# A convolution and an attention interleaved on one core: bound rows on the SyncE queue, a fourth convolution output tile, a new stored order

## Chip, cores and metric

The kernel runs on one core of one Trainium2 chip. The metric is the device time of one execution in microseconds; the kernel before takes 321.3 us (median of 3 runs, 320.46 to 322.23). The profile is one execution of the same kernel, with a span of 318.7 us.

## The reference

Two independent computations, whose outputs stand side by side in the last dimension (all inputs bf16, sequence S = 2048, width D = 640):

```python
def _A_ref(q, k, v, shift_k, ssm_k, ssm_D):          # H3 convolution
    k_shift = sum over t < 4 of k_pad[:, t:t+S] * shift_k[:, 3-t]
    kv = k_shift * v
    y = irfft(rfft(kv padded to 2S) * rfft(ssm_k padded to 2S))[:, :S]
    y = y.astype(bf16) + kv * ssm_D
    return q * y

def _B_ref(x, wq, wk, wv, wo, beta):                 # attention with memory
    # 32 heads of 20, N = 4 segments of L = 512 tokens
    for s in range(4):
        p = softmax(qs @ ks.T * scale + mask)
        a_dot = p @ vs
        a_mem = (phi(qs) @ M) / (phi(qs) @ z + 1e-6)
        outs[s] = g * a_mem + (1 - g) * a_dot        # g = sigmoid(beta)
        M, z = M + phi(ks).T @ vs, z + sum(phi(ks))
    return concat(outs) @ wo

return concatenate([a, b], axis=-1)
```

## The kernel before

**The convolution (A)** runs over five blocks dp of 128 channels. A Fourier transform is done as matmuls with constant tables (Wf forward, Wi inverse) and butterflies on VectorE. `load_sk` (388 to 396) brings the filter: GpSimd loads it into a buffer of the ring kT, VectorE copies it into a second order, and SyncE transposes that copy into another kT buffer; the ring has two buffers (n=2), so a copy has to wait until the last reader of the buffer two turns earlier is done. `load_kv` (398 to 407) brings v (tile vt, on GpSimd, on ScalarE for the first block) and the transposed k (tile kr, four transposes on SyncE). Then come `kshift` (diagonal matmuls, product with vt), the forward transforms "X" and "K" with butterflies `bfly`, `pointwise`, `ybfly`, and `inverse` (501 to 513): for each of four c it takes a tile from the ring outa, eight matmuls fill a PSUM bank, VectorE multiplies by q (tile qd, loaded by `load_q` on GpSimd) into outa, and GpSimd sends outa to HBM. Stage c of block dp is called A.dp.20 to A.dp.23 here.

**The attention (B)** runs over eight units u: segment s = u // 2 and half = u % 2 of the heads. A unit has a projecting part P.u and an attending part T.u. P loads xT once per segment (four transposes on SyncE; the first segment through TensorE), and projects K, Q and V in four token tiles of three blocks of five matmuls (128x320 each); ScalarE copies K and Q into the tile KQ, which SyncE transposes into KQT. `bound` (564 to 583) gets a bound of the softmax: a maximum over K (kam, VectorE), a matmul with the absolute values of Q (qabs), a copy by ScalarE into bT (16 x 512), and four transfers that put the rows of bT into row 20 of each head's 32 rows of KQT. So the matmul of Q and K subtracts the bound by itself. `mem` (585 on) updates the memory M. T has four groups g of four heads, `attn(g)`: matmuls into the single PSUM tile st (2048 wide), an exponential by ScalarE into ET, matmuls with V and the memory, a reciprocal rr and products on VectorE into o_s. For half 1 there follow `outt` (four transposes on SyncE, o_s to oT) and `outproj` (672 to 682), whose output GpSimd sends out.

**The order.** Nothing is issued while the functions run. The `Recorder` (100 to 273) keeps 1393 operations with their dependences; `emit` (197) then issues them in the order of the list ORDER (692, decoded in 756), a permutation of the 1393 indices packed as text. Each engine, and each engine's DMA queue, goes through its own instructions in that order, without overtaking; semaphores hold it where data is missing. Thus a DMA issued by SyncE waits in SyncE until its data is ready, and what stands behind it waits too. All instructions bear the line of `emit`, L216, in the profile, so groups are told apart by their tiles. `take` (225) gives the PSUM banks: one st tile and four banks w. `ring` (374) hands out the buffers in turn.

Of the kernel before, what the change touches and what calls it, by code (L numbers as in the profile page):

```python
# [21 lines left out]
S = 2048; D = 640; C = 512; P = 1024  # L22
H = 32; DH = 20; NS = 4; L = 512; NG = 8
# [252 lines left out]
class K3:  # L276
# [104 lines left out]
    def a_chunks(self, dp):  # L381
        nc = self.nc
        V = nc.vector
        dsl = slice(128 * dp, 128 * dp + 128)
        Wf, Wi, ident = self.Wf, self.Wi, self.ident
# [28 lines left out]
        def kshift(b):  # L414
            def f():
                kr, vt = st["kr"], st["vt"]
                ps = self.bank("w")
                for c in range(4):
                    for t in range(4):
                        cc = (c - t) % 4  # L420
                        p0 = KPAD + 128 * b + (c - t - cc) // 4
                        nc.tensor.matmul(ps[:, 128 * c:128 * c + 128], lhsT=kr[:, 0, cc, p0:p0 + 128], rhs=st["skd"][:, t, :], start=(t == 0), stop=(t == 3))
                V.tensor_tensor(out=vt[:, b, :, :], in0=ps.rearrange("p (c d) -> p c d", d=128), in1=vt[:, b, :, :], op=ALU.mult)
            return f
# [76 lines left out]
        def inverse(c):  # L501
            def f():
                U, qd = st["U"], st["qd"]
                outa = self.ring("outa", [128, 4, 128], n=3)
                py = self.bank("w")
                pyv = py.rearrange("p (a h d) -> p a h d", a=2, h=2)
                for h in range(2):
                    for k in range(4):
                        i, j = k // 2, k % 2
                        nc.tensor.matmul(pyv[:, :, h, :], lhsT=Wi[:, k, c, 128 * h:128 * h + 128], rhs=U[:, 4 * i + c, 256 * j:256 * j + 256], start=(k == 0), stop=(k == 3))  # L510
                V.tensor_tensor(out=outa[:], in0=py.rearrange("p (b d) -> p b d", d=128), in1=qd[:, :, c, :], op=ALU.mult)
                nc.gpsimd.dma_start(out=self.out[:, dsl].rearrange("(b p c) d -> p c b d", b=4, c=4)[:, c], in_=outa[:])
            return f

        X = [(load_kv, 0.1)] + [(kshift(a), 1.5) for a in range(4)] + [(fwd("X", c), 2.0) for c in range(4)] + [(bfly("X"), 7.0)]
# [4 lines left out]
    def b_proj_chunks(self, u):  # L520
        nc = self.nc
        V = nc.vector
        s, half = u // 2, u % 2
        KQT, PqT, Va = self.KQT[half], self.PqT[half], self.Va[half]
# [39 lines left out]
        def bound():  # L564
            kam = self.ring("kam", [128, 4], f32)
            V.tensor_reduce(out=kam[:], in_=KQT[:, 0:4, :], axis=AX.X, op=ALU.max, apply_absolute_value=True)
            A = self.ring("A", [128, 4, 16])
            V.tensor_tensor(out=A[:], in0=self.sel[:], in1=kam[:, :, None].to_broadcast([128, 4, 16]), op=ALU.mult)
            if s > 0:
                nc.scalar.activation(out=PqT[:], in_=QT, func=ACTF.Exp)  # L570
                tq = self.ring("tq", [128, 4, L])
                V.tensor_scalar(out=tq[:], in0=QT, scalar1=1.0, scalar2=1.0, op0=ALU.add, op1=ALU.max)
                V.tensor_tensor(out=PqT[:], in0=PqT[:], in1=tq[:], op=ALU.min)
            qabs = self.ring("tq", [128, 4, L])
            V.tensor_scalar(out=qabs[:].bitcast(i16), in0=QT.bitcast(i16), scalar1=0x7fff, scalar2=None, op0=ALU.bitwise_and)
            pb = self.bank("w")
            for g in range(4):
                nc.tensor.matmul(pb[0:16, :], lhsT=A[:, g, :], rhs=qabs[:, g, :], start=(g == 0), stop=(g == 3))
            bT = self.ring("bT", [16, L])
            nc.scalar.copy(out=bT[:], in_=pb[0:16, :])  # L580
            for hl in range(4):
                r = 32 * hl + DH
                nc.gpsimd.dma_start(out=KQT[r:r + 1, 4:8, :], in_=bT[4 * hl:4 * hl + 4, :])

        def mem():
            src, dst = self.Mbd[half][s % 2], self.Mbd[half][(s + 1) % 2]
# [10 lines left out]

        ch = [(load, 0.1)] if half == 0 else []
        ch += [(proj(t), 3.0) for t in range(4)] + [(bound, 4.0)]
        if s < NS - 1:  # L600
            ch.append((mem, 1.5))
# [88 lines left out]
BANKS = {"st": (1, 2048), "w": (4, 512)}  # L690
SUMMED = ("X",)
ORDER = (
    'c-jrs0|O9d8wJpNpXa{Wwr$(CZQJH*%WbuVp|;GSwrtzxmTg<#cmBkQWJDq)gd-YaArfLDB4Qvqq97_N0LX&KFa$(^5Zj_!WQ%F>5F3e625}J0Vp(*{geVrrVpvK`Zt*RZ#YGBBU~w&;'
    'Ww!j5(UMwbWU>O53P~)BB|u7~MO7rTbe7&yBZH;3+?LnUT4Kv%`7DQ}K?Y>CY?j8-Aw6<hE-Pe7FvJpCRun)HB(kE&hx{mnf+%R&Eh&<r5-Oq!Dx<I!v2s@4idr!%ZiP`6LoFAwAv<y-'
    '4{{(U$|Em&S#KL=eXOqyw-Q#;2H0pDZxyVf4YCO~#s*q36h}#vKxquNZ)~ddv&r^@^|xtO4qw|S`_4*Xij}d_R?5m+HGE}bZG?Sq<Lq0jfjU;#s-q?*Ssm0xE!0MQWW<m5ll^SB?XHcq'
    '={C{s*e&}3-(xZ+p^8<tR%nFQsAQF`4cekHTA&%KS#wmk8rB32tSK5=1JtyJXo(h94=t@eezBQ01+}cUb;Jw%VlS<p)wfS}&+Z$%3qIRCYmXV$4)bk+EwpFW0iDqa&8)foYQNbldtj}s'
    'k+rtQ_S7C)2kU5U>?gFfPWIZq#Xp#c@mPro=!)4k$G$^1%(A&Q6+Q6WR^Yw0vk%tZenu0UhL0A!sZB>je`1}ji~Rz5B>xc+ysO3V$R5RKAUWLMS#)28M@WIkc!H-`VoPlyW@0XW#Ud=S'
    'd01>qF&{Pkcl#X+@Q2m%KdrIPMmO7Fe_32_;&ag57UMT;v=z1lv(O8@(FZ*d+hckhkLU4ynI-V$))zgjr~QGy@F)7AKbB!2R$4-@?vHGXCGs~`!?)U7du&lXns2hzpeOYtp4gN5UEIS1'
    '+(&mjL@dVPM(o69TLbe=SY-`;o2|C3*lxQp0I__BJ;P4hhDM&&)A?F#$9inW25iCKwhlXx+@IquULu9Rz;2}UcX)+=Y>lP&*T~>&ZI``4Dqm+qP|x?EzBlmowio-*(g$NGcH2jQZT%DW'
    '82K69y|wSPy1vi8U<BIuerx9kEVUoB_TIurVi5kuAv<iX`~W)pejGy@@8KQ1r|0lqp3!r9SFi2eJd@Y)PTs{cdlrw)Y@XdCa2RT`I%~1Hcl0Bc%bWTsi^x8n+nafBKW%-zpAW}jKj260'  # L700
    'm>u*(UW3Q2s2B5re!@=L*WTa1@i8duk(kHx`XC?WgMEMx@qC`&zd{j@%raiqhx!pe=EMBB7xZs%9Lq5lqcFlp`f&fszeXXy;OG3JAN6ux+;4aZFYh<~yjSpRZmj6neY79N31sz>Udm76'
    'jGy+ie#IxabE04NtA5Jk@{U*XM_$<<`w#xW@A?#fkB9yN)BS}1>p%KbKk5JZG#77q;4{DERalLcSe1t`8b?r>hcONZF~)EESTEpJ{1ndMo}Wf(kHWKv%Bp_fYco1uc{INDYMxic^~6gk'
    'pPqVd<<U6*$s6!zAMbCx4ww2bKEvy>Az%ADfA8n;yBAd=7E@xTVG1txMy$uQOv&fI#6S2)f8mW;pD+C)&f@}RdOXJGxBiDGV{%g8xydC>^2z?E|K-2>GXD>SR9MUXZ@+{D{LK^clS5~$'
    '7r*#tpXI5Tnn{?HSM9uAvg<b6=lJ)YjztuM8JV6LSXS5UvR$wnHrLNu6VCIdJZEtfSM$9Yn=`-4C^J{^Uo7yLT<DAZA1|j&EU2IYilBBZuZoJSN{XTiYR{Ugt%$0lT8gCW=)jJwrrylO'
    '8_3B{?962>t<}E5tE#@1v$FoR|17GiD3)R?n(C^at{}OZs-*tbDqrb;bGer3AO54hjIJ1JtgC3lR&2o(x?+8J(JmvNO6e9_Grrb%TP9UAHCIfvP!ruobtO<sCR0l#)LL()l-leoluBDX'
    'gL1Hj5-G7(Dx+5EFaF7_T*_?B&TD9`cKU-it*zQ93vc3guGdCo(rRteI%QUBrO{e$P;Ta719f8(b!S(0VOpirI_70V<zo-#XF(QV7Hw5l_2VE8W`FKgS9Q}i?a+R0*8%O*PIcE|4dDQ0'
    'Qx6U0Kz3Fa?NN5E(N|on0UE)9I;NE@${Z@hoJy~rT*aPR&Es0bUh1trI-y+Zr(xXa-*7$qY6Fj`kxr_=Hu)$H(nt=`V13OI8qSd#s)!+kNa1Tm2;V417^WgTs^J>VaU9FS9K%yOt<Bn^'
    'Q97tG8m&W`sF>kfMGIpUJ(T2lj?;L3rSm$Y<2<W#D#Z!>f#0bZcWIqZ(q!%AZmsw4^@ED@1n-~(H~21I&=g%%c}~?d{j2{JH^dJKLK(&jmy|3d36~WoL=DNq_dLbK;ii&?TS^rwa5ATG'
    'f~Ko1r*ay1bDQtsW^UnaUC|xw<vwort9qfA+Uxr~ZJ5q$`jOX_I;0CfGkwSq(u5!NleY7THgZ3A`!CwTr`qG2cvo9_U-xu?+xSe+^*}p(r)LbA!e>q5w=B(x{EjDCjun|TWC@u=w(vzi'
    '>mU#Fp&sc7f8sB^%4@vL|9FY-)n32xJU{58uJ8~$=!RzUu{vr7XYrL@>y6&(0x$A9Kj~j)4>y=2Ae<$`X%-9TSUjBJR-esXevC)?EB~KvQ0SyZT+EyySD4Q^%pFpMJfToX848D+yu~}b'  # L710
    '&AVK{dwjyDoXf|I6%vNXAyJ4OqJ$zLZ^##lhVr3AC>ctH{GoJs#&;?Zp7RA?vP>u#Ua>-`5o(4RDjR01T$robsu(JVIjR)qX{l<3+M!DLRljKo_xmHx<3rBZeLmnUEo7ZgH&hMP!fRF!'
    'Z@579LjAB%4MM}vC@j(+TCCsor{3{B-_q;@8;2(0Bfqd|aQj5q68)vmY#Ew|U@bzc&@8kG5v*-!7up9It#ycK9YW{OF?0)^LYL4ZbPrua&(JIU57-o<i~'
)


# [73 lines left out]
```

The softmax here doesn't subtract the row's maximum and nothing guards it: scores larger than these inputs give would overflow.

## Time and profile before

| Engine | busy, us | share | instructions |
|---|---|---|---|
| TensorE matmul (PE) | 285.8 | 90% | 5182 |
| TensorE weight load (PEld) | 208.1 | 65% | 5182 |
| VectorE (DVE) | 249.0 | 78% | 382 |
| ScalarE (ACT) | 259.1 | 81% | 347 |
| GpSimd (POOL) | 79.8 | 25% | 138 |

The largest groups by tile, with the mean of one:

| Group | count | busy, us | mean, ns |
|---|---|---|---|
| ACT exponential, ET from st | 96 | 154.3 | 1608 |
| PE projection, w from wqkv and xT | 480 | 76.6 | 306 |
| ACT copy, F from w | 80 | 45.0 | 608 |
| DVE butterflies, S from S | 40 | 37.1 | 945 |
| GpSimd issue of the rows, KQT from bT | 32 | 16.3 | 515 |
| GpSimd issue of outputs, out from outa | 20 | 15.9 | 794 |

SyncE's instructions are only DMA issues and are listed as SPq. The DMA queue of SyncE moves 21.85 MB in 76,800 packets and takes 43.5% of the 16 DMA engines' span, that of GpSimd 12.42 MB and 15.6%. A share of busy time is a mean over the whole span. Three views go further: the waits (how long an engine stood and what came last), the chain (which work ended last, followed back), and windows (busy time of every engine within a stretch). "PEclk" is the clock that TensorE was granted, 1.00 being full speed.

### The profile page before, as it was taken

What the parts mean: (1) busy time and instruction counts of PE and PEld (TensorE: products, weight loads), DVE (VectorE), ACT (ScalarE), POOL (GpSimd) and SP (SyncE); (2) the same over time, 40 slices, a digit from 0 to 9 for tenths busy, and PEclk for the clock granted to TensorE, in tenths of its full rate; (3) what the DMA queues carried; (4) which work ended last, traced back from release to release, by engine and by line L of the source; (5) the groups of instructions that cost most, each with busy time, mean ns of one, the idle gap of its engine ahead of it and who ended that gap; (6) DMA issues with size and microseconds to landing.
All of it is one profiled execution on the core that took longest, in us unless ns stands there. A gap on an engine that the chain in (4) does not pass through costs nothing.

```text
span 318.7 us, 11778 instructions
## 1 busy us (share of the span) xinstructions
PE 285.8 (90%) x5182; PEld 208.1 (65%) x5182; DVE 249.0 (78%) x382; ACT 259.1 (81%) x347; POOL 79.8 (25%) x138
## 2 busy tenths in 40 slices
PE   0789999999999999989999999199999989997984
PEld 0456777787578776757777766147767766764662
DVE  0264847899948899999989599295998999999970
ACT  0466689999997999999889999349988999987722
POOL 8000302700350011217300228200042243112443
PEclk9999999999999999999999999769999999997999
DMA  8899497699851877856091799935029681111264
GB/s 256 226 197 216 109 154 100 166 241 150 120 151 33 105 113 132 132 98 167 23 152 23 116 169 136 127 97 70 2 86 147 124 149 45 40 40 51 78 149 140
DMA packets 88115, 38.51 MB, mean 121 GB/s; under 512 B 78768, under 2 KB 84960, under 8 KB 87936
## 3 DMA queue, kind: packets, MB, share of 16 engines
q1 hardware_dynamic: 76800, 21.85, 43.5%
q0 software_dynamic: 5424, 12.42, 15.6%
q10 hardware_dynamic: 5840, 3.49, 3.7%
q8 instruction: 40, 0.66, 0.9%
q14 instruction: 11, 0.09, 0.1%
HBM read 14.15 MB, written 5.24 MB: 61 GB/s over the span
## 4 chain that ended last, share of the span: by engine, by line
PE 55%; DVE 20%; DMA 10%; ACT 8%; issue 4%; ACTq 1%; POOL 0%; SPq 0%; POOLq 0%; DVEq 0%
PE w L216 47%; PE st L216 8%; DVE S L216 7%; ACT ET L216 5%; DMA kT<-kT 5%; DVE o L216 2%; DMA o_s<-in_B_x_dram 2%; DMA oT<-o_s 2%; DMA KQT<-KQ 2%; DVE kam L216 2%; DVE pr L216 1%; DVE outa L216 1%; DVE tq L216 1%; DVE Kh L216 1%; DVE rr L216 1%
## 5 line engine op out<-in xcount | busy, mean ns | idle before, releaser
L216 ACT ACTIVATE ET<-st 128x2048 bf16<-128x2048 f32 (+1 forms) x96 | 154.3, 1608 | 10.8 <-PE st L216 9.5
L216 PE MATMUL w<-wqkv,xT 128*128 128x320 bf16 x480 | 76.6, 306 | 2.2 <-DVE xT L216 0.9
L216 PEld LDWEIGHTS <-xT 128*128 128x128 bf16 x480 | 45.1, 100 | 25.0 <-issue 6.7
L216 ACT CAST F<-w 128x512 bf16<-128x512 f32 x80 | 45.0, 608 | 12.0 <-PE w L216 11.6
L216 PEld LDWEIGHTS <-Wf 128*128 128x128 bf16 x400 | 36.1, 98 | 19.2 <-DMA out_dram<-outb 7.6
L216 PEld LDWEIGHTS <-ET 128*128 128x128 bf16 x1280 | 40.1, 96 | 7.3 <-issue 5.6
L216 PE MATMUL w<-Va,ET 128*128 128x21 bf16 x1280 | 43.0, 173 | 0.7 <-DVE outa L216 0.5
L216 POOL DMA_DIRECT2D KQT<-bT x32 | 16.3, 515 | 99.5 <-ACT bT L216 50.9
L216 DVE TENSOR_TENSOR S<-S 128x2048 bf16<-128x2048 bf16 (+1 forms) x40 | 37.1, 945 | 0.2
L216 PE MATMUL w<-vt,Wf 128*128 128x256 bf16 x240 | 35.5, 273 | 0.1
L216 PE MATMUL st<-KQT 21*128 21x512 bf16 (+3 forms) x512 | 34.4, 297 | 0.0
L216 PEld LDWEIGHTS <-later 32*128 32x128 bf16 x1536 | 18.8, 92 | 23.5 <-issue 21.1
L216 ACT CAST KQ<-w 128x320 bf16<-128x320 f32 x64 | 26.2, 435 | 8.3 <-PE w L216 6.8
L216 PE MATMUL st<-later 32*128 32x32 bf16 (+1 forms) x1536 | 27.0, 180 | 6.1 <-ACT ET L216 5.5
L216 PE MATMUL w<-kT,Wf 128*128 128x256 bf16 x160 | 23.5, 280 | 8.3 <-DMA kT<-kT 7.4
L216 PE MATMUL w<-wo,oT 128*128 128x320 bf16 x160 | 26.6, 309 | 2.0 <-DVE o L216 1.9
L216 POOL DMA_DIRECT2D out_dram<-outa x20 | 15.9, 794 | 44.4 <-DMA xT<-in_B_x_dram 26.5
L216 DVE TENSOR_TENSOR S<-Xh,Kh 128x4096 bf16<-128x4096 bf16 x10 | 22.9, 2286 | 0.1
L216 DVE TENSOR_REDUCE kam<-KQT 128x4 f32<-128x2048 bf16 x8 | 18.2, 2278 | 5.8 <-DMA KQT<-KQ 5.8
L216 ACT CAST outb<-w 128x320 bf16<-128x320 f32 x32 | 13.3, 443 | 10.0 <-PE w L216 7.8
L216 PEld LDWEIGHTS <-oT 128*128 128x128 bf16 x160 | 15.3, 100 | 8.9 <-issue 2.7
L216 POOL DMA_DIRECT2D qd<-in_A_q_dram x20 | 15.1, 757 | 23.6 <-DVE outa L216 17.5
(74 smaller groups left out, 432.6 us busy)
## 6 DMA issues: line engine op xcount, KB each, us to landing
qd<-in_A_q_dram POOLq DMA_DIRECT2D x20, 128.0 KB, 3.9
out_dram<-outa POOLq DMA_DIRECT2D x20, 128.0 KB, 3.1
out_dram<-outb POOLq DMA_DIRECT2D x16, 160.0 KB, 2.4
vt<-in_A_v_dram POOLq DMA_DIRECT2D x16, 128.0 KB, 3.6
kT<-in_A_ssm_k_dram POOLq DMA_DIRECT2D x4, 512.0 KB, 4.2
Wf<-c_wf ACTq DMA_DIRECT2D x4, 256.0 KB, 6.6
Wi<-c_wi SPq DMA_DIRECT2D x1, 1024.0 KB, 6.5
wo<-in_B_wo_dram SPq DMA_DIRECT2D x1, 800.0 KB, 6.9
```

The lines of the kernel that those rows point to most:

```text
L216: f(*fargs, **fkw)
```

## The change

Three edits. The four row transfers at the end of `bound` are issued by SyncE instead of GpSimd, 32 of 4 KB in all; their work and data stay the same. The ring outa gets a fourth buffer, so that a product of `inverse` waits for the output transfer four turns earlier instead of three. And the stored order is another one. It contains the same 1393 operations, so that every engine but SyncE and GpSimd issues exactly as many instructions as before, at other places; among the differences are the place of the filter transposes kT in SyncE's queue, the first loads of ScalarE, and the interleaving of A and B towards the end.

```diff
@@ inverse(c) @@
-                outa = self.ring("outa", [128, 4, 128], n=3)
+                outa = self.ring("outa", [128, 4, 128], n=4)
@@ bound() @@
             for hl in range(4):
                 r = 32 * hl + DH
-                nc.gpsimd.dma_start(out=KQT[r:r + 1, 4:8, :], in_=bT[4 * hl:4 * hl + 4, :])
+                nc.sync.dma_start(out=KQT[r:r + 1, 4:8, :], in_=bT[4 * hl:4 * hl + 4, :])
@@ ORDER @@
-    'c-jrs0|O9d8wJpNpXa{Wwr$(CZQJH*%WbuVp|;GSwrtzxmTg<#cmBkQWJDq)gd-YaArfLDB4Qvqq97_N0LX&KFa$(^5Zj_!WQ%F>5F3e625}J0Vp(*{geVrrVpvK`Zt*RZ#YGBBU~w&;'
...
+    'c-jTQ0{|FQ6a~<G-@AXdZQHhO+qT)v8f&)g)lgdvHP*b^YPP+aJ13G6iI5Ok5DAW0h=C}GhNy@DASNOrpaKlh5g9^Ei)xWAw#7zV#6dKRZkdo7Q7n$duvnHDDJ_*Hw-grNQXw7^SX_%|'
...
```

More of the change, by code (lines that the diff above doesn't have):

```diff
@@ L692 @@
 ORDER = (
-    'c-jrs0|O9d8wJpNpXa{Wwr$(CZQJH*%WbuVp|;GSwrtzxmTg<#cmBkQWJDq)gd-YaArfLDB4Qvqq97_N0LX&KFa$(^5Zj_!WQ%F>5F3e625}J0Vp(*{geVrrVpvK`Zt*RZ#YGBBU~w&;'
-    'Ww!j5(UMwbWU>O53P~)BB|u7~MO7rTbe7&yBZH;3+?LnUT4Kv%`7DQ}K?Y>CY?j8-Aw6<hE-Pe7FvJpCRun)HB(kE&hx{mnf+%R&Eh&<r5-Oq!Dx<I!v2s@4idr!%ZiP`6LoFAwAv<y-'
-    '4{{(U$|Em&S#KL=eXOqyw-Q#;2H0pDZxyVf4YCO~#s*q36h}#vKxquNZ)~ddv&r^@^|xtO4qw|S`_4*Xij}d_R?5m+HGE}bZG?Sq<Lq0jfjU;#s-q?*Ssm0xE!0MQWW<m5ll^SB?XHcq'
-    '={C{s*e&}3-(xZ+p^8<tR%nFQsAQF`4cekHTA&%KS#wmk8rB32tSK5=1JtyJXo(h94=t@eezBQ01+}cUb;Jw%VlS<p)wfS}&+Z$%3qIRCYmXV$4)bk+EwpFW0iDqa&8)foYQNbldtj}s'
@@ L697 @@
[L697 to L712, printed above, removed]
+    'c-jTQ0{|FQ6a~<G-@AXdZQHhO+qT)v8f&)g)lgdvHP*b^YPP+aJ13G6iI5Ok5DAW0h=C}GhNy@DASNOrpaKlh5g9^Ei)xWAw#7zV#6dKRZkdo7Q7n$duvnHDDJ_*Hw-grNQXw7^SX_%|'
@@ new lines @@
+    'nJtMWwPY3_=`4$7w7izpGFdiDiPT7M8LTSOBB!N8LQ8FFERp4~+?L<cT4Kv%`K*BDvNXtmLRQ#{SUF38@>ao;pqKTwtjKN!EeCQUAM&H34YZ<G+=^Kt<U(!~K~WUOSSx@bRuJPX53->='
+    '@**jQ*>D?b$xs=UP!Uzo$NE|sl(3RE-ul@@%Z@=d*hX1@D~94Ii4quXlWe+uWixGpl|?y}vC>w`%Gv-MVbxFr-&$#mv2Uz8zP3762enWW=}{N8F~w$}6zbXxn`+Z+q}{X0cE_gRu6<|s'
+    'Z5pOxI;vPzYlTK=jY`%Sm8}h0pe<UW8LC-zn`Jeu2^v^aG_(e&X${dFEvz0|+82Y@$1AI6_3e|*wOW=DwQaV|vpLot9ncOB?4d2Q<+j4++eA#pc6^O)_y$`s39qf0HMh^!$llljYh??q'
+    'wLP-N*1;azTkD9G)(f4{2|X|ybI``xT1R_soopta*<xE{OKhoqhbGq4Uf4@(XYK7<^u{bi^v>4B<|2}Jwf7d;qxd}ZL?67s2m5H-@Xp+y;W?svay-QjJV6Sqv9-1oE3wL!VHH-}a?Hm9'
@@ new lines @@
+    'tiW2-^mVolwS2v8u*SX^du*e{^(Bxu@r788Zr0uQ+BRE*MTqV3JdSU&%@*Gic<>(9(>7rv`l25q_<C%>7R2=a7>EJbZci+sSNDCE$p5t(zTckOe-_oF`Hz;&lXzlJ>O1im578C((FG6i'
+    '2yqyT-9i7!_QQNHe#Fn%VLPp%e~(7~vmL}Qb_hdozz$kkkKyV3KfFUM-;F(Zji0a&Z?MIFKypvvL-7)?u+?_q7aYK0r1Vt&y`}fJ$lyQNA^R8ge3$)--FDd8`bU7j+9$MgvbBFkcmK_5'
+    'u&y7mFBpNNcFa<H4{zgX{J3@X+Ws3h;|Px7DC&D{jzj}*=`H+(owQay2%SAP>v%WM;q5)6=k%VQ$+LNL@94d}lXvjUJ{Vm*i}&@@$nFt148L10Z|dhPBKvr5Z|1%In4h-lJnny3EuONP'
+    'JmDw(ycP9gKG4tDSsRXi-rq<0Xdj2d9*KE8uMhG8KG=tNJ|E-xy@*F<887QY{dYg*!@QvX;iGX1<1q$f{eu62LVn5r^vizQ%Xx9X<t6+tFYmX#g5PlCd9Ua<eYk(+BYlLQ^D7>g_k5C<'
@@ new lines @@
+    '^oxGYvwA7N>ZSd<pFshi?3Mh9SN5mwyzkTfk<ak=c<dkWouBc)eU{Jkv;L2N>*5`M;Z^)B&f$SS^r~LXqw)gI<07IkunH@2EH2n_Ou+A`%&M%$Q8<BK{0b*A&hPqo&#gRq=6O|I&pn@J'
+    '`vjlkFTI5R^#-iN|NM==^|?OJ=ld&f$Y`v~iJpjw`Oc&By%$w6t@e0K!+K1?HJ+9!xz-zTo!94UZ_GdO!9RL@e(md>`o{l)$u-5N`Uc<V3w)FRgU!Chr375)30X*sJQ<TS6|YzlrsfqC'
+    'RuRSIRV$;U?9FL@3F(-g8F<rf*(Zm-ctLIDXWzoo+RRPt%f)`(F4~{=m(^AsU9uat#LH``SI{zV!lsO)xLWSb*qr$ll#zd<tTHnO%V~vI(@J0ETRjuEc`jZ?1XWZ`wPPg}P%TAN2i`;{'
+    'Mp9(mLUq;9HnwL+Mp0+(^s1__?Os<=RZp=LTha8l{bQ9?Mah*yO_h_;6+?}64R_FjC3P1~)J)gWTrIRoJAAXYYK!8j4O_7fZ`)N|v&&XW@zs{C*^){1y(dsIwNyg=;H{KW+muRe)mm-T'
@@ new lines @@
+    'PC1yHiIiBowOt!|59^toS$PB5xQ<zPnj5&54YWrY^pmGnM(t1<?bI$cR33I=Or=#<?(=lYqOAH^gP2JJxL1Sui!v)O^YI7nVty860TyL9CQ*8I=Rp3bt{TFl>Zae+kH>UG{n=dy)I-^H'
+    'Q2TXKL)lqf^sBP#dws<L`avT&P^Yw=IaGu>l}m-$lRMZ`JK0O$v$y)FpLTPvkLDhp*6%u_zB;Qy{6qcqqmSVr4dX}-(O`|@2o2{*MGPSfRirRV5yEK22*Wg7V>yB2IgXQfPUrQL_Gyfc'
+    'Yn;X^W;mhA`dZ@^EtKR0O;jmPWDkC&GmIX-(IM^fVw|F>I>^J??b9?}e=2IYs0;c_aYAuUXKC*D+t}lmG((qFo-_5WCh0p>;57cNL;Oc^L;R2+lwrJZMae>va8<LFINVm!kUZQ`s!*0w'
+    'IfFC#6A$w@|CLAlu72Y+-P1l^*Ac$bYwhKaOdG!CEZ)#f&C)rh4&O0dNFOqU+5Fj`>3|>QVV|S9dai^1i~s8PwVx05K*#tqU+ASOataUmS(e~re#5U>j*s*U5AY<@gva`wPc(;(bW3x2'
@@ L713 @@
+    'oF|wuWD40r=8!dH37_>v|L{6*@CvW;z5Zf*E#wD%R0l2M8@<&ZT)>X%q<{6Fo@zc%@e(idldkb^W)C^SO(I+*L$UBDZ?Sl=;9(vW&hr9q^Dgi39wUdGAxg*<5{6izP)HPFhr(eA^M({5'
+    'cSsrXgyk#}?(+ekaVhhK{NbHea1~dxXeb{_gp%PYONG+mISYh>p-gzemwd%HtPpC1nqjfZhH_zvmTH;isbW~5%Ar!2uUesYSg0yt4UhUmuH+*w*JCc@6E4zXu2-E<H&hMP!fU=|^-wRY'
+    'Q2nq{4MM}vDE!M+TC3Gsrw#g#ANZb)LzD24U)VG>3&B1S7Qx<ejW()zXc^2}g%-iBO=uT7hR&gFXdgb4);dHqS+~$BbO>ESkI+5z3|&L7@IM_MqKp'
 )
```

## Prediction, made before the changed kernel ran

> **What bounds the kernel now.** I read the shares of busy time first, then the waits of TensorE, then the chain that ended last, and last a table of windows around the longest hole. TensorE is busy for 285.8 of 318.7 us, so almost all that an order of work can win lies in the 33 us where it stands still. The waits of PE say where those are; after the start one wait stands out:
>
> ```profile
> PE 285.8 (90%) x5182; PEld 208.1 (65%) x5182; DVE 249.0 (78%) x382; ACT 259.1 (81%) x347; POOL 79.8 (25%) x138
> PEclk9999999999999999999999999769999999997999
> ...
> PE w L216 <- DMA kT<-kT: 7.4, 1, 7.4
> PE w L216 <- DMA ident<-c_ident: 7.3, 1, 7.3
> PE st L216 <- ACT ET L216: 5.5, 13, 1.0
> ```
>
> One matmul stood 7.4 us for one transpose of the convolution's filter (tile kT), and the granted clock dips in the same slices. The chain by time names the piece, and the timeline of the SyncE queue says why it was late (start, length, engine, operation):
>
> ```profile
> 193.23 14.58 DMA kT<-kT
> 207.94 3.85 PE w L216 x15
> ...
> 187.06 2.85 SPq L216 DMA_TRANSPOSE xT<-in_B_x_dram  x2
> 189.96 1.83 SPq L216 DMA_TRANSPOSE kr<-in_A_k_dram  x1
> 191.83 1.29 SPq L216 DMA_TRANSPOSE xT<-in_B_x_dram  x1
> 193.23 5.16 SPq L216 DMA_TRANSPOSE kT<-kT  x1
> ```
>
> The kT of block dp=3 stood behind the four kr of dp=4, the four xT of the last segment and two oT, which are needed later; its source was ready at 174.95 (the VectorE copy of that tile). It was issued at 193.23 and landed 14.6 us later, where the tile's median is 5.1. The table of windows (PE, PEld, DVE, ACT, POOL busy, granted clock, DMA share, GB/s) shows the hole and its surroundings:
>
> ```profile
> 150.00:172.00 22.00, 21.97 (x429) 16.53 (x425) 19.78 (x38) 19.80 (x28) 3.15 (x6) 1.00 0.38 71
> 184.00:200.60 16.60, 16.04 (x324) 11.35 (x323) 15.78 (x22) 15.68 (x19) 8.11 (x14) 1.00 1.15 139
> 200.60:208.00 7.40, 0.06 (x1) 0.09 (x2) 0.95 (x3) 1.09 (x2) 2.30 (x3) 0.64 1.20 152
> 208.00:216.00 8.00, 8.00 (x82) 4.35 (x83) 7.21 (x9) 4.35 (x8) 0.00 (x0) 0.69 0.25 70
> 216.00:228.00 12.00, 11.08 (x282) 9.28 (x280) 8.89 (x15) 11.92 (x13) 0.00 (x0) 1.00 0.34 46
> 244.00:304.00 60.00, 53.64 (x1099) 38.02 (x1097) 58.66 (x77) 52.95 (x60) 16.91 (x26) 0.97 0.39 82
> ```
>
> From 200.6 to 208 all engines stand still at once: no other engine used the hole. The DMA share is over 1 before and in it and only 0.38 at 150 to 172. From 216 to 228 ScalarE is full, and from 244 to 304 VectorE is (58.66 of 60 us): there PE no longer bounds.
>
> **What the skill says.** The page "DMA: Bandwidth & Descriptors", section "Issuing engines are not separate DMA queues", says that all issuing engines feed the same 16 DMA engines. The trace agrees: the 14.6 us landing falls where SyncE's transposes and GpSimd's loads of vt and qd ran together (share 1.15 to 1.20). In "Anatomy of one DMA — SWDGE (gpsimd) path" it says that a semaphore wait happens on the issuing sequencer, so a row that waits on SyncE holds all behind it. The trace shows this on GpSimd, which waited 50.9 us for bT ahead of the row transfers. "TensorE: Matmul & The Clock Gate", "What's actually happening", gives half clock after an idle window of about 3.4 us; the trace agrees, with half clock from 202.6 to 212.9.
>
> **The change part by part.** I set the two stored orders beside each other, engine by engine, and put the durations of the trace before on the new positions. Every engine has the same instructions.
>
> Order, kT of dp=3. Its VectorE copy goes 11.2 us of VectorE work earlier, to about 164 to 167, where it waits for the last matmul that reads the other kT buffer (dp=2, about 165). Its transpose now stands after the KQT of unit 5 and the four kr, ahead of all xT and the oT of that stretch. Issue at about 167 plus 3.4 (median issue of kT) plus up to 5.1 (median landing) gives 170 to 176, against 200.6 when PE needs it. Even the worst landing seen, 14.6, ends at 185. So the 7.4 us go, and with them VectorE's 6.4 us wait for vt, which lay in the same hole. Why not more, as the half clock from 208 to 212.9 goes too and cost PE 2.45 us? Because of ScalarE: from its exponential at 194.66 to that at 225.83 it has 23.5 us of work in 31.2 us, so 7.7 us is all that can be closed up. The gain is 7.4 to 7.7; I take 7.7. After that VectorE bounds, with 93.4 us of work left before and 93.8 after from the same point (T.4.3): the tail shifts as a whole.
>
> Order, start. ScalarE issues seven loads instead of nine before it loads its table (each 0.7 to 1.1 us), so the table load begins near 7, not 8.54, and the first projection near 10.5 instead of 11.91: 1.4 us. Against this the memory update P.0.6 now follows P.0.4 at once and waits about 1.6 us for the copies of KQ and Va; of PE work, one projection block (five matmuls of 306 ns, 1.5 us) is done earlier by then. Between +1.4 and -0.2, I take 0.7.
>
> Rows on SyncE. 32 transfers at 515 ns leave GpSimd: 16.3 us of its 79.8, on an engine that sits idle 75%, so nothing of itself. On SyncE each costs 0.4 to 0.7 us of issue (its plain loads), some 18 us in a queue that waits 69.5 us for PE st and 46.6 us for o_s. The cost is in the queue. Unit 0's rows hold two KQT and the first xT of unit 1; unit 1's stand behind the KQT of unit 2; unit 4's fourth row waits for the KQT of unit 5 (released at 160.1) and one kr, so it is issued at about 162.7 and lands near 166 (GpSimd's rows take 2.6 us), against 168.8 for the exponent that reads it; unit 6's last three wait for the KQT of unit 7 (released at 235.5), land near 239, and are needed at 242.4. The tightest margins are 3 us. Queueing costs 0 to 4 us where a landing goes the way of the worst KQT (10.9 us against a median of 3.3, so 7.6 later); I take 0.4, for two short holes.
>
> Other moves, the kT of dp=1 and dp=4, Wi, vt and qd: each lands 3 to 25 us ahead of its use by the same reckoning, except qd of dp=3, whose three loads stand behind an output transfer on GpSimd at about 261.6, land at 269 to 270 and are needed at 270: 0 to 0.5, I take 0.2.
>
> Fourth outa. Three buffers cost one wait, at the very end: VectorE 3.0 us for the output transfer of A.4.20. The chain that ended last does not run through it (there PE is the last, from 306.02). 0.
>
> Sum: -7.7 - 0.7 + 0.4 + 0.2 = -7.8, from the middle time of 321.3: 313.5.
>
> **Rivals.** (1) A wait takes the removed one's place: slower. For it: SyncE is the queue that caused the stall (16 transposes without pause from 172 to 207), and it now also carries eight waits for bT. If the three tight groups (units 1, 4, 6) land 7.6 us late, past margins of 3 to 3.6, each costs about 4 us: 12, less the gain of 8.4, is +3.6, so 325. Against it: 150 to 172, where the kT goes, has a DMA share of 0.38, and two of the three groups lie in stretches of 0.4. (2) The hole closes but the tail takes part of it: the last 60 us are full on VectorE (58.66), the order of PE and VectorE there is changed too, and a late qd or vt (before 6.4 us for vt) costs 3 to 4 us: about 317. (3) All comes at once: 7.7, all of the 1.4 at the start, and 2 us of the 5.5 us that PE loses in 13 short waits for ET: 310. (4) SyncE's rows cost as much as the kT gains: within 1.6 us of 321.3.
>
> **How the numbers follow.** The main case, 311.5 to 315.5, has a chance of 0.52; case 2 (to 319.5) 0.15, case 3 0.11, case 4 0.07, case 1 0.15. Faster by over 0.5% is 0.52 + 0.15 + 0.11 = 0.78. The predicted time is the main case, 313.5. The range runs from 309.0 (case 3 with its lower edge) to 320.5; above it lie case 1 and a half of case 4, below it little.
>
> **What would show it.** The waits of PE should have no wait for kT above 1 us. The clock should stay at 1.00 around 195 to 215 and the DMA share of that stretch fall under 1. First projection at about 10.5. In the SyncE queue's waits a new row of rows (KQT) on ACT bT, with no exponent waiting for a row for more than 1 us. The stretch in which VectorE is full should have its old length, begun 8 us earlier. The prediction is wrong if PE st or the PqT waits for KQT grow by more than 3 us, or if VectorE's tail is longer than before by what the hole gave.

## The result, and the profile after

The changed kernel takes 310.2 us (median of four runs, 309.5 to 311.9), the kernel before 321.8 us (four runs, 320.5 to 323.4): a ratio of 0.965, with a 95% interval of 0.958 to 0.971. A second set on another chip gave 310.8 (five runs, 310.5 to 312.4) against 321.3, a ratio of 0.966 (0.963 to 0.970). Ratios and their intervals leave out runs over 1.5% above the fastest of the same kernel, medians do not, so where the kernel before spreads widely its ratio shows a smaller gain than the medians. The prediction was 313.5, range 309.0 to 320.5: right in direction and inside the range, but the measured time is 3.3 us lower, outside the main case of 311.5 to 315.5.

The page after, from the busy shares, the clock and the waits of PE, answers to the first fence of the prediction:

```profile
PE 282.2 (92%) x5182; PEld 207.5 (67%) x5182; DVE 251.6 (82%) x382; ACT 258.8 (84%) x347; POOL 64.9 (21%) x106
PEclk9999999999999999999999999999999999999999
...
PE w L216 <- DMA ident<-c_ident: 7.2, 1, 7.2
PE st L216 <- ACT ET L216: 4.8, 12, 1.0
PE w L216 <- DVE o L216: 2.9, 3, 1.4
```

The wait for kT is gone and nothing has come in its place: the longest wait of PE after its start is 1.4 us. GpSimd has lost 15 us of work, VectorE and ScalarE have the same work in a shorter span. The timeline of the SyncE queue (start, length, operation) shows why; the kT now comes ahead of every xT:

```profile
163.85 2.58 SPq L216 DMA_TRANSPOSE kr<-in_A_k_dram  x2
166.54 1.34 SPq L216 DMA_TRANSPOSE kT<-kT  x1
171.90 2.53 SPq L216 DMA_TRANSPOSE oT<-o_s  x2
```

It is issued at 166.5 instead of 193.2, and the first matmul that reads it, at 196.3, does not wait. When it landed is not in this trace; in the same order with the rows on GpSimd, where it is, it took 5.7 us from its issue (14.6 in the kernel before). The windows (PE, PEld, DVE, ACT, POOL busy, clock, DMA share, GB/s) of the stretches that answer to those of before, some 3 us earlier up to the hole and 12 after it:

```profile
184.00:196.00 12.00, 12.00 (x244) 8.32 (x242) 10.57 (x16) 11.25 (x17) 7.98 (x11) 1.00 0.65 163
196.00:204.00 8.00, 7.77 (x132) 5.45 (x130) 7.79 (x9) 7.71 (x11) 0.00 (x0) 1.00 0.81 124
204.00:216.00 12.00, 11.66 (x285) 9.45 (x281) 11.52 (x19) 12.00 (x15) 0.00 (x0) 1.00 0.33 46
232.00:292.00 60.00, 52.49 (x1095) 37.92 (x1095) 58.18 (x77) 52.23 (x60) 15.02 (x21) 1.00 0.38 77
```

PE is busy without a hole, the clock stays at 1.00, the DMA share falls from 1.15 to 0.65 and 0.81 (1.02 between 192 and 200). The 60 us in which VectorE is full are there again with the same length and the same work, only begun 12 us earlier.

**Where the 11 us of the profiled span (318.7 to 307.7) come from.** Comparing the n-th matmul of one trace with the n-th of the other gives PE's lead at each place: 2.1 us from 43 us on, 2.0 at 176; 3.1 at 198, just ahead of the hole; 12.4 at 218 to 223; 13.2 near 300; 11.0 at the end. So: start -2.1, ahead of the hole -1.0, hole -9.3, tail -0.8, the last few us +2.2. The two orders differ, so the n-th matmul is not always the same piece of work: between 43 and 190 us the lead has a median of 2.1, but single values from 0.4 to 4.0. The hole stands clear of that and so does the start by its median, the small terms do not.

### The profile page after: what moved, and what is told of

Read it like the earlier page. It is cut to its first block, busy times and chain, and to the rows that moved or that the text cites. A ratio compares the mean times of both kernels' runs of the same rounds, so it can differ in the third digit from the quotient of the medians.

```text
span 307.7 us, 11766 instructions
## 1 busy us (share of the span) xinstructions
PE 282.2 (92%) x5182; PEld 207.5 (67%) x5182; DVE 251.6 (82%) x382; ACT 258.8 (84%) x347; POOL 64.9 (21%) x106
## 4 chain that ended last, share of the span: by engine, by line
PE 58%; DVE 14%; ACT 13%; issue 6%; DMA 4%; POOL 2%; SPq 1%; POOLq 0%; ACTq 0%; DVEq 0%
PE w L216 49%; ACT ET L216 9%; PE st L216 9%; DVE S L216 5%; POOL out_dram L216 2%; DMA ident<-c_ident 2%; DMA KQT<-KQ 2%; DVE Kh L216 1%; ACT F L216 1%; DVE Xh L216 1%; ACT Va L216 1%; DVE vt L216 1%; DVE outa L216 1%; ACT KQ L216 1%; DVE pr L216 1%
## 5 line engine op out<-in xcount | busy, mean ns | idle before, releaser
L216 PE MATMUL w<-wqkv,xT 128*128 128x320 bf16 x480 | 77.5, 305 | 1.1 <-DVE xT L216 1.1
L216 PEld LDWEIGHTS <-xT 128*128 128x128 bf16 x480 | 44.2, 99 | 22.9 <-issue 4.6
L216 ACT CAST F<-w 128x512 bf16<-128x512 f32 x80 | 45.7, 608 | 1.8 <-PE w L216 1.2
L216 PEld LDWEIGHTS <-Wf 128*128 128x128 bf16 x400 | 35.9, 98 | 10.5 <-issue 4.8
L216 POOL DMA_DIRECT2D vt<-in_A_v_dram x16 | 12.3, 774 | 112.1 <-PE w L216 109.1
L216 PE MATMUL w<-wo,oT 128*128 128x320 bf16 x160 | 25.4, 299 | 2.6 <-DVE o L216 2.5
L216 PE MATMUL w<-S,Wi 128*128 128x256 bf16 x160 | 20.5, 273 | 1.9 <-DVE S L216 1.6
```

The lines of the kernel that those rows point to most:

```text
L216: f(*fargs, **fkw)
```

## The experiments

Lines of code that were added to reorder operations have the form: take operation i out of the list and put it ahead of operation j. Where two kernels are compared, each ratio is to the kernel before on the same chip.

### The stall: place in the queue or crowding

One operation of the old order moved, the kT transpose of dp=3, ahead of the KQT transposes of unit 5:

```diff
     order = np.frombuffer(...).tolist()      # old order, three outa, rows on GpSimd
+    order.remove(371)                        # A.3.10, kT transpose
+    order.insert(order.index(1099), 371)     # P.5.2, KQT transpose
```

> The kernel before with one operation moved: the kT transpose of dp=3 on SyncE goes ahead of the KQT transposes of unit 5's third and fourth tile, so it is issued at about 176 instead of 193. Queue theory (the place in SyncE's queue made the stall): it lands before 191, the 7.4 us wait is gone, and with the half clock 9 to 10 us are gained: about 312. Congestion theory (too many transfers between 184 and 208, whatever their order): vt's piece, which landed at 207.31 beside kT, holds VectorE and then TensorE in kT's place, and 0 to 4 us are gained: 318 to 322.

Measured: 312.7 us (four runs, 312.3 to 314.7) against 320.8 (15 runs), ratio 0.982 (0.973 to 0.991). The interval is wide because the kernel before itself varied between 315.7 and 322.2 on this chip, of which more below. The two profiles show it place by place: 310.8 us of span against 318.7, with PE 1.0 us behind at 198 and 8.6 ahead at 218. The timeline and the tile's landing:

```profile
175.84 1.80 SPq L216 DMA_TRANSPOSE kT<-kT  x1
...
DMA to landing us min/median/max: 3.7/5.3/7.5
```

So in the profiles one operation of 1393 brings 7.9 of the 11.0 us; the medians say 8.0, the ratio about 5.7. The moved kT itself landed after 5.5 us. VectorE's wait for vt did not take its place.

The other half of the old queue's trouble, three kr transposes ahead of unit 5's second KQT, with kT left behind the xT:

```diff
+    for i in (430, 431, 432):                # A.4.0, kr
+        order.remove(i)
+        order.insert(order.index(1089), i)   # P.5.1, KQT transpose
```

> The kernel before with the other half of the change in that queue: three kr transposes of dp=4 move ahead of unit 5's second KQT, to 161 to 166, and kT keeps its place behind the xT. Queue theory: kT is issued about 5 us earlier (three transposes of 1.3 to 1.8 us), at 188, and is still late unless its landing falls from 14.6 to under 12; 2 to 9 us gained, 312 to 319. Congestion theory: with three transposes out of the crowded stretch all landings there come back to the medians (5.1 us for kT), the stall is gone whole: 312.

Measured: 313.7 (312.5 to 316.2), ratio 0.985 (0.975 to 0.995). The kT was issued at 191.03, only 2 us earlier than in the kernel before, and still landed in time: it took 9.0 us instead of 14.6. Hence the place alone is not the whole cause; with three transposes taken from the stretch the landing was shorter as well. Either cure suffices.

The converse, in the changed kernel: the three kr and the kT put back behind the last xT.

```diff
+    for i in (430, 431, 432, 371):
+        order.remove(i)
+        order.insert(order.index(1207), i)   # P.6.1, KQT transpose
+    ...                                      # the next filter's load on GpSimd moved behind it
```

> The changed kernel with the three kr and the kT of dp=3 put back where the old order had them in SyncE's queue, behind the last xT (here also behind the rows of unit 5); the load of the next filter on GpSimd follows the kT. Converse of the first experiments. If the place in that queue is worth the 9 us at 200 us that the traces show: 7 to 10 us slower than the changed kernel, 317 to 320, with a wait of TensorE for kT or kr near 197 to 205 and a dip of the clock after it. If the emptied GpSimd queue has cured it by itself: within 2 us.

Measured: 317.1 (317.0 to 317.3), against 310.8 for the changed kernel on the same chip; ratio 0.986 (0.983 to 0.990). The timeline of SyncE and the waits of PE:

```profile
185.23 3.98 SPq L216 DMA_TRANSPOSE xT<-in_B_x_dram  x3
191.04 2.43 SPq L216 DMA_DIRECT2D KQT<-bT  x4
193.52 3.76 SPq L216 DMA_TRANSPOSE kr<-in_A_k_dram  x3
197.39 3.21 SPq L216 DMA_TRANSPOSE kT<-kT  x1
...
PE w L216 <- DMA kT<-kT: 5.9, 1, 5.9
```

The matmul that waits for the kT starts at 202.62, so the kT landed about 5.2 us after its issue: no long landing here, the place alone makes the stall. It was issued at 197.4 and needed at 196.8. PE falls back by 7.5 us there and keeps that to the end. So a late enough place makes the stall by itself, and an early place takes it away.

### The half clock after the stall

The prediction let ScalarE cap what the end of the half clock could bring at 0.3 us. To keep TensorE warm and leave the stall, discarded matmuls go ahead of the stalled one, into the bank that it fills:

```diff
                     pf = self.bank("w")
+                    for n in range(38 if (dp, kind, c, i) == (3, "K", 0, 0) else 0):
+                        nc.tensor.matmul(pf[:, 0:512], lhsT=Wf[:, 0, 0, 0:128], rhs=Wf[:, 1, 1, :], start=True, stop=True)
```

A first kernel had 28 of them.

> The kernel before with 28 extra matmuls of 128x512 into the bank that the stalled matmul is about to fill, ahead of it, so that TensorE is busy with discarded work for about 6 us of the 7.4 us hole; their sums are overwritten, nothing else changes. It keeps the clock at full speed and leaves the stall. If the half clock after the stall cost time to the end: about -2 us, 319.5. If ScalarE's work between 194.66 and 225.83 bounded the recovery as the prediction had it: -0.3, 321.3. If the extra matmuls delay the stalled one: slower.

It took 319.1 against 320.8 in the median, a ratio of 0.999 (0.994 to 1.004); one of its twelve runs took 1448 us, for a reason that is not known. It tells nothing of the question: kT landed later in its profile (at 209.4), TensorE still idled 2.5 us, and half clock followed all the same (0.60 from 211 to 215).

> The kernel before with 38 instead of 28 discarded matmuls of 128x512 ahead of the stalled one, some 8.4 us, so that TensorE does not idle at all (with 28 it still idled 2.5 us, and a clock of 0.73 followed at 212 to 216). Read in the trace, from the first real matmul after the hole to the st of T.5.1, which took 11.8 us before at half clock: about 9.5 if the half clock cost its 2 us or more, 11.5 if ScalarE bounds this stretch. The time of the run follows by less, since the extra matmuls end up to 1 us after the transpose lands.

With 38 the hole is filled (windows of this kernel):

```profile
200.60:209.00 8.40, 8.40 (x48) 3.80 (x40) 2.42 (x5) 1.02 (x1) 2.33 (x4) 1.00 1.21 148
209.00:212.00 3.00, 3.00 (x44) 1.71 (x42) 2.97 (x4) 1.45 (x3) 0.00 (x0) 1.00 0.53 158
212.00:216.00 4.00, 3.58 (x75) 2.68 (x73) 2.76 (x3) 4.00 (x7) 0.00 (x0) 1.00 0.08 18
```

The clock stays at 1.00, and from the first real matmul (208.88) to the st of T.5.1 (218.57) it takes 9.7 us, where the kernel before takes 11.8 (207.94 to 219.73; the timelines of TensorE, first before, then with 38):

```profile
207.94 0.58 PE L216 MATMUL w<-kT,Wf 128*128 128x256 bf16 x2 [7.39 <-DMA kT<-kT]
219.73 0.30 PE L216 MATMUL st<-later 32*128 32x64 bf16 x16 [0.24 <-ACT ET L216]
```

```profile
208.88 0.38 PE L216 MATMUL w<-kT,Wf 128*128 128x256 bf16 x2
218.57 0.30 PE L216 MATMUL st<-later 32*128 32x64 bf16 x16 [0.25 <-ACT ET L216]
```

So the half clock cost 2.1 us, and ScalarE does not hide them: the cap was wrong. The time of the run, 320.3 against 320.6 (ratio 1.001, 0.999 to 1.003), doesn't show the gain, since the extra matmuls themselves end 0.9 us late and most of the remaining lead of 1.2 us is lost again between 290 and 298 us, where the clock is halved for 6.8 us (288.8 to 295.6) and in the kernel before for 3.4 (291.4 to 294.8). Its 20 runs lie within 2.1 us (319.2 to 321.3), the 39 of the kernel before within 9.8: the extra matmuls fill the stretch in every execution, also in those in which the kT may have landed early, so the two medians do not compare the half clock alone.

### The two edits of the code without the new order

```diff
-                outa = self.ring("outa", [128, 4, 128], n=3)
+                outa = self.ring("outa", [128, 4, 128], n=4)
...
-                nc.gpsimd.dma_start(out=KQT[r:r + 1, 4:8, :], in_=bT[4 * hl:4 * hl + 4, :])
+                nc.sync.dma_start(out=KQT[r:r + 1, 4:8, :], in_=bT[4 * hl:4 * hl + 4, :])
```

> Only the two code edits (rows on SyncE, fourth outa) in the old order. If the rows hold what stands behind them on SyncE (the rival that ended slower): over 322, with new waits of TensorE or VectorE for KQT, xT or kr behind bT. If the edits alone bring part of the gain (GpSimd's loads of vt and qd no longer behind rows, so less crowding around 195): 314 to 319. By the prediction (0.4 for rows, 0 for outa): 321.2, within the spread of the kernel before, 315.7 to 322.2.

Measured: 318.2 (20 runs, 315.3 to 322.7) against 320.6 (39 runs, 315.9 to 325.7); ratio 0.994 (0.991 to 0.998). A gain of 2 us, in times that lie in two heaps, eight runs from 315.3 to 316.9 and twelve from 318.1 to 322.7. The profile was of the first heap, and there the stall is all but gone although the kT is issued even later than before (timeline of SyncE and waits of PE):

```profile
194.10 3.42 SPq L216 DMA_TRANSPOSE kT<-kT  x1
PE w L216 <- DMA kT<-kT: 0.4, 1, 0.4
```

The matmul that waits for the kT starts at 202.56, so the kT landed about 8.4 us after its issue, not 14.6. In this run GpSimd issued its first qd load at 193.60, after one vt load; in the kernel before the first qd and the second vt load went out at 191.12 and 191.87, ahead of the kT. With the three kr moved, too, the kT (191.03) went ahead of the first qd load (191.80), and landed after 9.0 us. That suggests that what gets in first decides how long the kT takes; it is read from three traces and was not forced by an experiment.

The changed kernel with the rows back on GpSimd (the second edit undone, order and outa as changed):

> The changed kernel with the rows back on GpSimd, same order. By the prediction the rows cost 0.4 on SyncE, so 310 or a little under. If the order relies on a GpSimd free of rows (vt, qd, kT loads and output transfers behind 16.3 us of issues and waits for bT): 312 or more, with VectorE waiting for vt or qd.

Measured: 312.6 (312.3 to 315.1), ratio 0.978 (0.973 to 0.984), against 0.965 and 0.966 for the changed kernel: some 2 us slower by the medians (310.2 and 310.8, each on another chip). The timeline of GpSimd in this kernel, and in the changed kernel:

```profile
193.15 2.01 POOL L216 DMA_DIRECT2D KQT<-bT  x4 [9.88 <-ACT KQ L216]
195.16 0.17 POOL L216 MEMSET kr<- 128x64 bf16 x1
195.24 0.79 POOL L216 DMA_DIRECT2D out_dram<-outa  x1
196.01 0.77 POOL L216 DMA_DIRECT2D vt<-in_A_v_dram  x1
```

```profile
188.21 0.77 POOL L216 DMA_DIRECT2D vt<-in_A_v_dram  x1 [3.01 <-PE st L216]
188.97 1.49 POOL L216 DMA_DIRECT2D qd<-in_A_q_dram  x2
```

With the rows GpSimd stands 9.9 us for unit 5 and starts the loads of v at 196.0 instead of 188.2; TensorE then waits 0.5 us for vt, and has lost 0.7 us at 205. The rest of the 2 us is not settled: the profiled spans, 310.5 and 310.6 in the second set of the changed kernel, don't show it.

### The start

The old order with its first operations taken from the new order, once 206 of them, once 181 and together with the kT move:

```diff
+    first = other[:181]                      # other: the new order
+    order = first + [i for i in order if i not in set(first)]
+    order.remove(371)
+    order.insert(order.index(1099), 371)
```

> The kernel before with only the first 206 operations in the order of the changed kernel (to about 43 us), the rest in the old order; rows still on GpSimd. The trace of the changed kernel is 2.1 us ahead at that point. If the start is a term of its own: -2.1, about 319.5. If it is taken back by a later wait (the kT stall is set by SyncE's queue, not by TensorE): near 0, 321.5. By the prediction's number: -0.7, 321.

> The kernel before with the kT transpose moved as in the first experiment (which gave 312.7 against 320.8) and with the first 181 operations, to about 41 us, in the order of the changed kernel; at that number the two orders differ in only two operations, so that the seam is clean (at 206 it was not: the trace lost there 3.6 us between 26 and 54 us). If the start is a term of its own that lasts to the end: 2 us less than the kT kernel, about 310.7, and TensorE 2 us ahead of it from 43 us on. If a later wait takes it back: 312.7. If the seam costs again, TensorE's lead is lost before 60 us and nothing follows about the start.

Measured: 324.7 (ratio 1.019, 1.010 to 1.027) for the first, 312.4 (ratio 0.977, 0.971 to 0.982) for the second, where the kT move alone had 312.7 (0.982). In both TensorE was 2.2 to 2.4 us ahead at 26 us and had lost it all by 54 us, and the first kept the stall (its kT landed 15.8 us after its issue). As said beforehand, in this case nothing follows about the start: its lead is real in the changed kernel, but these seams throw it away, and it was not shown that it can be had without the rest of the new order.

### The fourth outa in the new order

The changed kernel with three outa buffers. The new order has some operations ahead of what a third buffer must wait for; there the missing output transfer is pulled ahead.

```diff
-                outa = self.ring("outa", [128, 4, 128], n=4)
+                outa = self.ring("outa", [128, 4, 128], n=3)
+    ...                                      # an operation's missing predecessors are issued just ahead of it
```

> The changed kernel once more, unedited, as the measure for the three others on the same chip: 0.96 to 0.97 of the kernel before, with the same waits as in its first profile. Its time spread over 309.5 to 311.9 with the mean clock (1.000 to 0.981), so a profile with a dip of the clock in the last 60 us should show a span of 309 to 310 instead of 307.7.

> The changed kernel with three outa buffers; an operation that the new order has before one of its predecessors pulls that one ahead of itself, so that some output transfers of the convolution are issued earlier on GpSimd; all else keeps the order. By the prediction (fourth outa worth 0): the time of the changed kernel within 0.5. If the order lives on late output transfers: 1 to 4 us slower, with VectorE waiting for out_dram from outa, or GpSimd's loads behind outputs.

Measured: 310.8 for the unchanged one, 313.8 (312.0 to 315.0) for three buffers; ratios 0.966 (0.963 to 0.970) and 0.976 (0.971 to 0.980). Up to 295 us TensorE with three buffers keeps within 0.2 us of the first profile of the changed kernel. The loss is all at the end (timeline of VectorE with three buffers, then with four in that first profile):

```profile
298.88 0.69 DVE L216 TENSOR_TENSOR outa<-w,qd 128x512 bf16<-128x512 f32 x1 [2.58 <-DMA out_dram<-outa]
299.49 0.68 DVE L216 TENSOR_TENSOR S<-S 128x1024 bf16<-128x1024 bf16 x1
```

```profile
296.72 0.69 DVE L216 TENSOR_TENSOR outa<-w,qd 128x512 bf16<-128x512 f32 x1 [0.20 <-PE w L216]
297.32 0.68 DVE L216 TENSOR_TENSOR S<-S 128x1024 bf16<-128x1024 bf16 x1
```

In the new order the product of A.4.23 stands on VectorE ahead of the last butterfly of A.4.19, on which the last inverse (A.4.22) hangs. With three buffers that product waits 2.6 us for an output transfer, the butterfly behind it comes 2.2 us later, and TensorE with it (4.0 us of waits for S in all, against 1.6). A half clock from 301.2 to 304.6 adds to it in this profile. In the old order nothing of VectorE stood behind the same wait.

The unchanged kernel's second profile has a span of 310.6, a little over the 309 to 310 that was expected, with a mean clock of 0.981, where the first had 307.7 with 1.000. TensorE is 0.6 us behind from 43 to 276 us, some 2 at 283 and 2.9 at the end. In between it had half clock, from 278.6 to 285.4 (windows of the second profile):

```profile
276.00:280.00 4.00, 2.28 (x66) 1.83 (x66) 3.97 (x5) 3.27 (x2) 3.53 (x5) 0.82 0.40 112
280.00:284.00 4.00, 4.00 (x34) 1.85 (x32) 3.93 (x6) 2.74 (x4) 0.00 (x0) 0.50 0.23 65
```

### A try at a faster kernel

VectorE is full in the tail and GpSimd is not. Fifteen additions into o_s go to GpSimd:

```diff
-                    V.tensor_tensor(out=o_s[...], in0=o4[:, :, 0], in1=o4[:, :, 1], op=ALU.add)
+                    (nc.gpsimd if u >= 4 and (u, g) != (7, 3) else V).tensor_tensor(out=o_s[...], in0=o4[:, :, 0], in1=o4[:, :, 1], op=ALU.add)
```

> The changed kernel with eleven... fifteen of the additions into o_s (128x320 bf16, 0.32 us each on VectorE; units 4 to 7 without the very last) on GpSimd, in the same places of the order. A try at a faster kernel: from 232 to 292 VectorE is full (58.2 of 60 us) while GpSimd is at 15. If VectorE bounds the tail and GpSimd takes under 2 us for one: 1.5 to 3 us faster than the changed kernel. If GpSimd's additions wait behind output transfers in its queue, so that the oT transposes start late, or slow VectorE beside them: no gain, or 1 to 4 us slower.

Measured: 315.3 (314.0 to 316.0), 4.5 us slower than the changed kernel on the same chip. The tile o_s:

```profile
L216 POOL TENSOR_TENSOR o_s<-o x15: 786/1244/1774, 195.5 to 295.1; 128x320 bf16<-128x320 bf16 x15
L216 DVE TENSOR_TENSOR o_s<-o x9: 317/324/917, 130.6 to 295.2; 128x320 bf16<-128x320 bf16 x9
```

An addition takes 1.24 us there instead of 0.32, which is within what was allowed for; but TensorE, set beside the first profile of the changed kernel, loses 0.5 us near 205 and 5 us between 250 and 298, in part while its clock is halved (277.4 to 287.6, longer than in the second profile). Whether it is the queue (the additions wait 44 us in all for their operand, and output transfers behind them) or a slower VectorE beside a busy GpSimd was not separated. None of these kernels beats the changed one.

## Why the prediction was right, and where it was off

**The stall** (predicted -7.7; measured -9.3 in the trace; with the one moved operation -9.6 at the hole, -8.1 by the medians and about -5.7 by the ratio). The mechanism was right in its main steps: late issue behind transposes that are needed later, an early free stretch, a hole that closes. That crowding made the landing long remains argued, for the DMA share does not order the landings (last section). The size was not right. The step that failed is ScalarE's cap: "23.5 us of work in 31.2 us, so 7.7 us is all that can be closed up". The 23.5 us is a sum of durations, and on ScalarE the listed durations overlap: the next instruction mostly starts 0.1 to 0.2 us before the last one's end, as here in the kernel before:

```profile
220.29 1.97 ACT L216 ACTIVATE ET<-st 128x2048 bf16<-128x2048 f32 x1
222.07 1.99 ACT L216 ACTIVATE PqT<-KQT 128x2048 bf16<-128x2048 bf16 x1
223.87 1.96 ACT L216 ACTIVATE ET<-st 128x2048 bf16<-128x2048 f32 x1
```

Counted once, the same 25 instructions occupy 21.0 us, so the stretch could close by 10.2. In the changed kernel it takes 21.3 us, 9.9 less. The 2 us of half clock that the prediction wrote off for that reason came back in full, as the filled hole shows: 11.8 us against 9.7. Two readings were loose without harm. The 5.1 us of landing count from the start of the issue, so the 3.4 of issue was counted twice; the transposes of kT alone landed after 5.0 to 7.7 us, the stalled one apart. And the half clock began at 202.7, 2.1 us after TensorE's last matmul had ended (200.55), so the trace bears out that half clock came with the hole, but not the figure of about 3.4 us of idle that the prediction cites.

**The start** (predicted -0.7, in the trace -2.1). The first projection starts at 10.64, as forecast (10.5). The wait ahead of the memory update was priced at 1.6 us and cost about 0.8; and TensorE's other early waits (for KQ, Va and wqkv) shrank instead of staying. From the first projection to the second st (42.54 before, 40.41 after) the same number of matmuls takes 29.8 us instead of 30.6. The experiments could not isolate this term.

**Rows on SyncE** (predicted +0.4). No wait for a row appeared: SyncE's waits put 5.3 us on bT, in two waits, a row took 0.57 us of its time, and no engine waits for KQT from bT. The margins of 3 us held. By the times the sign is wrong. "GpSimd sits idle 75%, so nothing of itself" overlooked what the prediction itself had read of SyncE: a queue that waits holds what is behind it. On GpSimd that was the loads of vt and qd, and taking the rows away lets these start 7.8 us earlier. With the new order this is worth some 2 us by the times, of which the trace shows 0.7; the rest stays open.

**Fourth outa** (predicted 0). By the trace true of the old order, where the 3.0 us wait is not on the chain; not of the new one, where three buffers cost 3.0 us in the medians. The prediction judged an edit by the order that it was to replace.

**qd and the tail.** The holes of 0.2 for qd did not appear. In the tail VectorE bounds for 60 us as before, as forecast. Not foreseen: the clock can dip there, as in the kernel before at 291.4 to 294.8 and in the second profile of the changed one, which fell 2.3 us behind the first from 276 us on. The mean clock was 0.981 to 0.987 in seven of nine executions of the changed kernel; where it dipped is known for the profiled one alone. The first profile happens to have no dip, so part of its 11 us of span is that; the times contain both kinds. Nor did the tail shift wholly: the last few us give back 2.2 us of the lead, for a cause that was not looked for.

Rival 1, a new wait, is refuted: the DMA share in the stretch fell and the margins held. Rival 2, a tail that takes part of the gain, came in a small part only: 13.2 us of lead near 300 become 11.0, and no late qd or vt shows. Rival 3, all at once, came nearest with 310, by luck: its 2 us from the waits for ET did not come (4.8 instead of 5.5), and it was the half clock that filled the sum. Rival 4, rows that cost as much as the kT gains, did not come.

## What to carry to other kernels

When one engine stands 7 us for one transfer, look first at the queue that issued it, and only then at the transfer: ask what stood ahead of it that is needed later, and when its source was ready. To cap a gain by an engine's work, count its occupied time once and not the sum of listed durations. And judge a buffer or a queue in the order that it will serve: the same wait was free in one order and cost 3 us in the other.

## What the runs showed of the hardware

- The same transpose (the kT of dp=3) took very different times from issue to landing, and the mean DMA share from 2 us before to 6 us after its issue does not order them: 14.6 us at a share of 1.22 (kernel before), 15.2 at 1.19 (hole filled), 15.8 at 1.01 (first 206 operations new), but 9.0 at 0.98 (three kr moved), 8.4 at 1.04 (the two edits alone) and 5.2 at 1.27 (the converse). The last two are read from the matmul that waited for it.
- The kernel before spreads from 315.7 to 325.7 us; the kernel with the kT moved, with four executions, within 2.4, and the one with the hole filled, with 20, within 2.1. That the spread comes from the landing of the kT fits this, but is not shown: only one execution of the kernel before was profiled.
- TensorE's half clock began 2.1 us after the last matmul in the kernel before, and followed an idle of only 2.5 us with 28 discarded matmuls. In the second profile of the changed kernel it began at 278.6, although TensorE had been busy for 2.59 of the 3.40 us before, with no gap over 0.45; in the first profile it was busy for 2.04 of the same 3.40 us, and the clock stayed at 1.00. Inside the runs each half clock lasted 3.4, 6.8 or 10.2 us.
- SyncE's own time to issue a transpose of kT ranged from 1.34 us (changed kernel, at 166.5) to 5.89 (hole filled, at 193.1). Here, too, the DMA share around it does not decide: 2.23 us at 1.23 (changed kernel, at 131.1), 3.27 at 0.73 (first 206 operations new, at 246.8).
